# Attention and a mixing layer in one kernel: transposes moved from TensorE to VectorE blocks and DMAs

## Chip, cores and metric

The kernel runs on one core of a Trainium2 chip. The metric is the device time of one execution in microseconds (us). Its engines are TensorE (PE; its weight loads are shown as PEld), VectorE (DVE), ScalarE (ACT), GpSimd (POOL) and SyncE (SP), which issues nearly all DMAs. Each engine takes its instructions strictly in order.

## What is computed

Eight batches, eight heads, 1152 keys and 576 pooled queries of 64 numbers. The attention's output, put together to 576 x 512 for each batch, is x of a mixing layer:

```python
q_pool = q.reshape(B, H, S // 2, 2, D).mean(axis=3)
scores = scale * np.matmul(q_pool, k.transpose(0, 1, 3, 2))
scores = scores - np.max(scores, axis=-1, keepdims=True)
attn = np.exp(scores)
attn = attn / (np.sum(attn, axis=-1, keepdims=True) + 1e-09)
x = np.matmul(attn, v)            # then (B, 576, 512)

theta = x @ w_theta               # 512 x 512
zr, zi = x * np.cos(theta), x * np.sin(theta)
y = einsum('ts,bsd->btd', w_tok_r, zr) + einsum('ts,bsd->btd', w_tok_i, zi)
u = x + y
return u + np.maximum(u @ w_ch, 0.0)
```

q, k and v are 32-bit, the four weight matrices 64-bit floating point; products are formed from a high and a low part of each operand (three products each).

## The kernel before

**First part (attention).** The work is cut into 32 pairs (a batch and two heads). For a pair, `load_q`, `load_k` and `load_v` bring the inputs, `prep_t` transposes keys and pooled queries on TensorE, `prep_hi` (ScalarE) and `prep_lo` (VectorE) split them. `maxpass` and `max_tail` form rough scores with a product of the high parts, and VectorE reduces each to its maximum: queries lie in four blocks of 128 with both heads side by side, and the last 64 queries of both heads in one tile `tail`. `max_nm` takes the maxima's negative, `max_row` transposes them on TensorE and copies them to `mT`, and `load_max` puts them by four DMAs into one row `nmr` for each head. `escore` then forms the exact scores with that row added, ScalarE takes the exponential into `pc`, `ssum` adds those up on GpSimd, `av` multiplies with `vn`, and `norm_sum` to `norm_store` divide by the sum (through DRAM, to spread a row over the partitions) and store the transposed x of the pair to `xd`. Between these steps a generator, `weights`, reads the four weight matrices, which arrive as 64-bit floating point, and converts them piece by piece (`narrow`, then `square` or `token`), nine steps a pair at `W_AT`.

**Second part (mixing).** For each of eight batches `xload` brings the transposed x (512 x 576, in four chunks `c`), with the last 64 columns twice, so that the tokens fill five tiles `j` of 128. `xhi` and `xlo` split it. For each tile `xturn` transposes x back on TensorE (four transposes into the bank pxn), `theta` forms twelve products, and `chain` makes cosine and sine of it in eight steps on ScalarE and VectorE, multiplies them with x, and splits the result into Z (nine tiles; the last holds cosine and sine of the last 64 tokens). `token_mix` forms y in two groups of chunks, `uadd`, `uhi` and `ulo` make u, `channel` and `relu` the last product for the output's chunk `e`. The result stands transposed in `uT`; `oturn` transposes it on TensorE (four transposes into po for each of five tiles), `ocopy` copies it out and `ostore` writes it.

**Order.** Everything is put on a list with a position and sorted: in the first part in units of one score step (18 a pair, `PLAN`, `PREP_AT`, `MAX_AT`, `W_AT`), in the second in units of about a microsecond (56 a batch, `THETA_AT`, `CHAIN_AT`, `TOK_AT`, `CH_AT`, `OT_AT`). Each engine, SyncE too, takes its instructions in this order. In the first part all PSUM tiles share four slots of two banks that `bank2` gives out by a forecast (`HOLD`); in the second there is one bank each for theta (`h`) and for transposes (`t`), four `m` and two `r`. A tile with several buffers waits until the last user of the buffer is through.

Of the kernel before, what the change touches and what calls it, by code (L numbers as in the profile page):

```python
# [20 lines left out]
MAX_AT = (-25.08, -24.951, -24.126, -21.989, -17.714, -16.703, -16.481, -16.035, -13.864, -10.761, -9.027, -7.903)  # L21
SS_LAG = 5.493
AV_AT = (((10.593, 9),), ((19.957, 9),))
PREP_AT = {'t0': -34.901, 'hi0': -34.757, 'px': -9.4, 'lo0': -34.733, 't1': -26.381, 'hi1': -26.225, 'lo1': -25.86, 'tail': -25.662, 'row': -7.096}
NS_AT = 29.431
AV_WORK = 0.49
W_FIRST = (9.45, 9.5, 9.85, 10.5, 12.75, 18.0, 18.6, 19.25, 20.45)
W_AT = (4.835, 9.561, 10.424, 11.959, 14.518, 18.485, 19.386, 19.73, 26.978)
W_LAST = (9.4, 10.2, 11.0, 11.8, 12.6, 13.4, 14.2, 15.0, 15.8, 16.6, 17.4, 18.2, 19.0, 19.8, 20.6, 21.4, 22.2, 23.0, 23.8, 24.6)
W_END = 30  # L30
PRO = ((-34.75, -25.8, -18.2), (-6.0, -5.0, 3.15), (3.75,))
MAX_AT0 = (-25.75, -25.25, -24.75, -24.25, -24.15, -23.25, -22.0, -21.95, -21.75, -21.25, -20.75, -20.25)
MAX_AT1 = (-18.663, -17.319, -17.013, -16.938, -15.662, -12.596, -12.521, -11.476, -9.96, -9.477, -8.761, -8.295)
PLAN = {'load_q': -55.68, 'load_k': -42.082, 'pool_q': -40.682, 'load_max': -4.09, 'load_v': 0.076, 'max_nm': -7.805, 'norm_spread': 33.352, 'norm_load': 35.388, 'norm_recip': 37.458, 'norm_save': 39.746, 'norm_bcast': 45.007, 'norm_out': 46.788, 'norm_store': 60.302}
# [3 lines left out]
HOLD = {'e': (3.508, 'a', 0.849), 'pm': (0.312, 'd', 2.851), 'pt': (8.399, 'ad', 1.03), 'px': (2.27, 'd', 2.445), 'pa': (8.509, 'a', 2.216), 'mt': (3.434, 'a', 1.931), 'ns': (2.931, 'a', 0.172), 'pw': (1.991, 'ad', 0.781)}  # L38
# [8 lines left out]
XN0_BANK = "tmmrt"  # L47
# [21 lines left out]
OT_AT = (57.8, 60.7, 61.2, 63.0, 68.5)  # L69
OT_LAG = 1.0  # L70
# [12 lines left out]
def pooled_attention_moe_kernel(  # L83
# [49 lines left out]
    xd = [dram.tile([DM, SQ], F32, name=f"xd{b}") for b in range(B)]  # L133

# [44 lines left out]
    def xhi(b, c):  # L179
        if b == 0:  # L180
            nc.vector.tensor_copy(xhl[0][c], bst[b]["xT"][:, c])
        else:
            nc.scalar.copy(xhl[0][c], bst[b]["xT"][:, c])

    def xlo(b, c):
        getattr(nc, ENG2["xlo0" if b == 0 and c < ND - 1 else "xlo"]).tensor_tensor(
            xhl[1][c], bst[b]["xT"][:, c], xhl[0][c].bitcast(F32), ALU.subtract
        )

    with ExitStack() as p1:  # L190
# [107 lines left out]
        def maxpass(i):  # L298
# [4 lines left out]
            for j in range(4):  # L303
                for g in range(3):
                    pm = bank2("pm", f"pm{i}_{j}{g}")
                    for h, hs in enumerate(HEADS):
                        nc.tensor.matmul(  # L307
                            pm[:, h, 0:W],
                            hi[hs, Q0 + j * P : Q0 + (j + 1) * P],
# [12 lines left out]
                    if rest:  # L322
                        nc.vector.tensor_reduce(mx[:, 8, 2:3], pm[:, 0, W:], AX.X, ALU.max)
                    yield

        def max_tail(i):
# [3 lines left out]
            for n, c, k, w in ((0, 0, 0, 4), (1, 0, 4, 2), (1, 2 * P, 6, 2)):  # L330
                nc.tensor.matmul(  # L331
                    pm[:, n, c : c + w * P], tl, hi[:, K0[k] : K0[k] + w * P], start=True, stop=True
                )
            nc.vector.tensor_reduce(mx[:, 8, 0:2], pm, AX.X, ALU.max)

        def max_nm(i):
            st = state[i]
            nm = st["nm"] = sml.tile([P, KT], F32, tag="nm", name=f"nm{i}")
            nc.vector.tensor_reduce(nm, st["mx"], AX.X, ALU.max, negate=True)

        def max_row(i):
            st = state[i]
            px = bank2("mt", f"pmt{i}")
            nc.tensor.transpose(out=px[0:KT, 0, 0:P], in_=st["nm"], identity=ident)
            mT = st["mT"] = sml.tile([KT, P], F32R, tag="mT", name=f"mT{i}")
            nc.scalar.copy(mT, px[0:KT, 0, 0:P])
# [304 lines left out]
        def plan(i):  # L651
# [10 lines left out]
            if i == 0:  # L662
                at(-7.8, 3, max_row, i)
# [340 lines left out]
```

## Time and profile before

| | before |
|---|---|
| three runs | 1379.57 us median (1379.42 to 1379.85) |
| the profiled execution | 1378.9 us |
| its span, first to last instruction | 1377.1 us |
| TensorE busy | 1336.4 us (97%), 12178 products |
| VectorE, ScalarE, GpSimd busy | 840.2, 699.2, 910.8 us |
[...]
| DMA | 132057 packets, 111.66 MB |

The first part ends about 873 us into the span. A row of the profile names the line of the kernel, the engine, the operation, and the tiles as out<-in. In a timeline the first number is the start and the second the time from the first start to the last end of the merged instructions, in us; TensorE's products are pipelined and their ends are modelled, so lengths are best read from one start to the next.

### The profile page before, as it was taken

How to read it: one execution, taken by the hardware profiler on the slowest of the kernel's cores; microseconds unless marked ns; L12 is line 12 of the kernel's file. 1: busy time of each engine (PE TensorE's matmuls, PEld its weight loads, DVE VectorE, ACT ScalarE, POOL GpSimd, SP SyncE). 2: the span in 40 equal slices, each digit the busy share in tenths (PEclk: the TensorE clock that was granted, in tenths of full speed). 3: DMA queues.
4: the chain of work that ended last, by engine and by line, in shares of the span. 5: the costliest groups of instructions: out<-in, count | busy, mean ns of one | idle time of the engine just before them, and what ended most of it. 6: DMA issues, size and time to landing. Idle time of an engine off the chain costs nothing.

```text
span 1377.1 us, 29856 instructions
## 1 busy us (share of the span) xinstructions
PE 1336.4 (97%) x12178; PEld 1087.0 (79%) x12178; DVE 840.2 (61%) x1143; ACT 699.2 (51%) x1250; POOL 910.8 (66%) x672
## 2 busy tenths in 40 slices
PE   4999999999999999999999999899999999999998
PEld 3777777777777777677677777588999999999998
DVE  5767776677767676777667765366254353625442
ACT  1556555565555655556555565365454444445341
POOL 1699899899989899889988989553241323323220
PEclk9999999999999999999999999999999999999999
DMA  4333433434433344243443313211121111111011
GB/s 104 101 95 105 124 96 92 129 95 105 122 103 103 96 130 105 74 126 95 120 120 99 88 52 103 74 70 39 36 60 52 36 39 35 39 35 52 23 35 35
DMA packets 132057, 111.66 MB, mean 81 GB/s; under 512 B 96192, under 2 KB 96576, under 8 KB 131920
## 3 DMA queue, kind: packets, MB, share of 16 engines
q1 hardware_dynamic: 131744, 109.29, 29.2%
q8 instruction: 96, 1.57, 0.5%
q0 software_dynamic: 176, 0.46, 0.1%
q14 instruction: 41, 0.34, 0.1%
HBM read 88.30 MB, written 21.27 MB: 80 GB/s over the span
## 4 chain that ended last, share of the span: by engine, by line
PE 82%; DVE 6%; ACT 5%; POOL 4%; issue 1%; DMA 1%; SPq 0%; POOLq 0%; ACTq 0%; DVEq 0%
PE pe L372 21%; PE pa L398 19%; PE py L834 11%; PE pth L756 7%; PE pm L307 7%; PE pr L873 6%; PE pt L267 4%; POOL ss L384 3%; PE pns L419 2%; PE px L331 1%; DVE mx L319 1%; PE pxn L744 1%; DVE r L778 1%; DVE r L779 1%; PE po L896 1%
## 5 line engine op out<-in xcount | busy, mean ns | idle before, releaser
L384 POOL TENSOR_TENSOR ss<-ss,pc 128x576 f32<-128x576 f32 x384 | 557.4, 1452 | 47.3 <-ACT pc L375 21.3
L319 DVE TENSOR_REDUCE mx<-pm 128x2 f32<-128x768 f32 x384 | 360.9, 951 | 184.2 <-PE pm L307 167.1
L375 ACT ACTIVATE pc<-pe 128x576 f32<-128x576 f32 x576 | 343.7, 654 | 82.6 <-PE pe L372 77.4
L398 PE MATMUL pa<-pc,vn 128*64 128x288 f32 x2304 | 293.5, 409 | 4.3 <-ACT tail L290 2.2
L807 POOL TENSOR_TENSOR Z<-ab,Z 128x512 fp32r<-128x512 f32 x40 | 51.6, 1291 | 310.2 <-ACT Z L803 267.8
L398 PEld LDWEIGHTS pa<-pc,vn 128*64 128x64 f32 x2304 | 159.7, 137 | 115.8 <-issue 5.9
L834 PE MATMUL py<-wtk,Z 128*128 128x288 f32 x1728 | 242.0, 297 | 0.0
L834 PEld LDWEIGHTS py<-wtk,Z 128*128 128x128 f32 x1728 | 233.2, 189 | 1.5 <-ACT Z L803 0.2
L372 PE MATMUL pe<-hi 64*128 64x288 f32 x1152 | 177.9, 301 | 0.7 <-DVE wtk L166 0.3
L372 PE MATMUL pe<-nmr,oner 64*128 64x288 f32 x1152 | 172.7, 291 | 2.9 <-DMA nmr<-mT 2.9
L372 PE MATMUL pe<-hi,lo 64*128 64x288 f32 x1152 | 173.2, 292 | 0.0
L372 PE MATMUL pe<-lo,hi 64*128 64x288 f32 x1152 | 173.0, 293 | 0.0
L307 PE MATMUL pm<-hi 64*128 64x384 f32 x768 | 146.6, 389 | 5.7 <-DVE mx L319 2.3
L372 PEld LDWEIGHTS pe<-hi 64*128 64x128 f32 x1152 | 110.7, 185 | 10.8 <-issue 6.5
L410 ACT COPY xu<-pa 128x288 f32<-128x288 f32 x64 | 25.6, 399 | 178.8 <-PE pa L398 178.8
L372 PEld LDWEIGHTS pe<-nmr,oner 64*128 64x128 f32 x1152 | 111.5, 185 | 3.2 <-DMA nmr<-mT 3.1
L307 PEld LDWEIGHTS pm<-hi 64*128 64x128 f32 x768 | 72.6, 188 | 51.3 <-issue 28.3
L372 PEld LDWEIGHTS pe<-hi,lo 64*128 64x128 f32 x1152 | 111.2, 185 | 0.0
L372 PEld LDWEIGHTS pe<-lo,hi 64*128 64x128 f32 x1152 | 110.9, 185 | 0.0
L873 PEld LDWEIGHTS pr<-us,wch 128*128 128x128 f32 x768 | 104.4, 188 | 2.0
L873 PE MATMUL pr<-us,wch 128*128 128x288 f32 x768 | 105.6, 295 | 0.0
L384 POOL TENSOR_TENSOR ss<-pc,pc 128x576 f32<-128x576 f32 x64 | 94.3, 1473 | 6.6 <-ACT pc L375 6.6
(97 smaller groups left out, 1659.0 us busy)
## 6 DMA issues: line engine op xcount, KB each, us to landing
qn<-in_q_dram SPq DMA_DIRECT2D x32, 576.0 KB
kn<-in_k_dram SPq DMA_DIRECT2D x64, 288.0 KB
vn<-in_v_dram SPq DMA_DIRECT2D x32, 576.0 KB
dn<-ro SPq DMA_DIRECT2D x64, 144.0 KB
xd<-xu SPq DMA_DIRECT2D x32, 288.0 KB
xT<-xd SPq DMA_DIRECT2D x8, 1152.0 KB
out_dram<-on SPq DMA_DIRECT2D x23, 192.0 KB
out_dram<-on SPq DMA_DIRECT2D x23, 128.0 KB
```

What stands on the lines that cost most here:

```text
L267: nc.tensor.transpose(out=pt[:, n, c : c + R], in_=src.rearrange("p h d -> p (h d)"), identity=ident[0:R, 0:R],)
L307: nc.tensor.matmul(pm[:, h, 0:W], hi[hs, Q0 + j * P : Q0 + (j + 1) * P], hi[hs, K0[3 * g] : K0[3 * g] + W], start=True, stop=True,)
L319: nc.vector.tensor_reduce(mx[:, j : j + 5 : 4, g : g + 1], pm[:, :, 0:W], AX.X, ALU.max)
L372: nc.tensor.matmul(pe[:, h, 0:HALF], w[hs], x[hs], start=(n == 0), stop=(n == 3))
L375: nc.scalar.activation(pcs[u, kt], pe[:, :, 0:HALF], AF.Exp, scale=SC)
L384: nc.gpsimd.tensor_tensor(st["ss", u], first, st["pc"][u, kt], ALU.add)
L398: nc.tensor.matmul(pa[hs, 0, 0:HALF], st["vn"][:, h, kt, :], st["pc"][u, kt][:, h, :], start=(kt == 0), stop=(kt == KT - 1),)
L419: nc.tensor.matmul(px[a : a + 32, 1, 0:HALF], ones, sets[u][n][:, h, :], start=(n == 0), stop=(n == len(sets[0]) - 1), tile_position=(0, a),)
L756: nc.tensor.matmul(th, xs[c][:, j * P : (j + 1) * P], ws[:, c], start=(n == 0), stop=(n == 11))
L807: engine("zlo", b).tensor_tensor(Z[1], t, Z[0].bitcast(F32), ALU.subtract)
L834: nc.tensor.matmul(st["py", c, u][:, 0:HALF], Z[zi][:, c * P : (c + 1) * P], wtk[wi][:, kw, u * HALF : (u + 1) * HALF], start=(i == 0 and ...
L873: nc.tensor.matmul(pr[u][:, 0:HALF], wch[wi][:, c, e * P : (e + 1) * P], st["us", ui][:, c, u * HALF : (u + 1) * HALF], start=(n == 0), st ...
```

## The change

- The second part's transposes of x: each pair's finished x is also transposed on VectorE in blocks of 32 x 32 (`norm_turn`, tile `xb`) and stored to a second DRAM buffer `xbd`. `xnload` reads it from there with four DMAs for a tile, whose pieces are 32 words (128 bytes) long, straight into `xn`. `xturn` and the copies of its bank are gone.
- The output's transposes: for all batches but the last, `oblock` transposes each finished chunk `e` on VectorE in blocks (28 times) and stores it with four DMAs of 128-byte pieces. `oturn`, `ocopy` and `ostore` stay for the last batch.
- theta's last tile holds 64 tokens of an even batch and 64 of the odd one behind it. It is formed in the even batch; its angle is kept in `r4`, and two DMAs make a copy with the halves changed over (`r4s`). In odd batches `theta` returns at once for j = 4, and high and low parts are made for 512 columns.
- The maxima: the query blocks are taken with a step of four, so that `load_max` can read the row straight from `nm`, four words a partition. `max_row` (a transpose, a ScalarE copy) is gone. The product of the tail with the last keys moves from the last step of `maxpass` to `max_tail`, in a PSUM tile of its own.
- Weights: in `narrow` two VectorE passes are gone; ScalarE does one pass more. Ten steps a pair instead of nine, and the transposes of `token` have a place of their own (`TURN_AT`).
- All positions of the first part and the forecast of its PSUM slots are new. Positions of the second part stay, but for the removed and added steps.

```diff
@@ first part, places
-MAX_AT = (-25.08, -24.951, -24.126, -21.989, -17.714, -16.703, -16.481, -16.035, -13.864, -10.761, -9.027, -7.903)
-SS_LAG = 5.493
+MAX_AT = (-25.047, -24.524, -21.303, -19.913, -17.966, -17.199, -16.59, -13.533, -11.031, -9.109, -7.944, -7.783)
+SS_LAG = 5.544
...
-PLAN = {'load_q': -55.68, 'load_k': -42.082, 'pool_q': -40.682, 'load_max': -4.09, 'load_v': 0.076, 'max_nm': -7.805, 'norm_spread': 33.352, 'norm_load': 35.388, 'norm_recip': 37.458, 'norm_save': 39.746, 'norm_bcast': 45.007, 'norm_out': 46.788, 'norm_store': 60.302}
+PLAN = {'load_q': -54.727, 'load_k': -43.238, 'pool_q': -43.609, 'load_max': -3.244, 'load_v': -11.696, 'max_nm': -7.412, 'norm_spread': 32.09, 'norm_load': 34.755, 'norm_recip': 36.124, 'norm_save': 36.922, 'norm_bcast': 37.251, "norm_out": 46.61, "norm_turn": 46.640, 'norm_store': 56.838}
...
-XN0_BANK = "tmmrt"
+XN_AT = -4.0
...
-OT_AT = (57.8, 60.7, 61.2, 63.0, 68.5)
-OT_LAG = 1.0
+OB_LAG = 0.1
@@ xload
-        nc.sync.dma_start(xT[:, :, SQ : 5 * P], xv[:, :, 4 * P : SQ])
+        if b % 2 == 0:
+            xw = xd[b + 1].rearrange("(c p) s -> p c s", p=P)
+            nc.sync.dma_start(xT[:, :, SQ : 5 * P], xw[:, :, 4 * P : SQ])
+
+    def xwide(b):
+        return slice(0, 4 * P if b % 2 else 5 * P)
@@ maxpass
-                            hi[hs, Q0 + j * P : Q0 + (j + 1) * P],
+                            hi[hs, Q0 : Q0 + 4 * P].rearrange("d (p j) -> d j p", j=4)[:, j],
...
-                    rest = j == 3 and g == 2
-                    if rest:
-                        nc.tensor.matmul(
-                            pm[:, 0, W:], st["tail"], hi[:, K0[8] : K0[8] + P], start=True, stop=True
-                        )
...
-                    if rest:
-                        nc.vector.tensor_reduce(mx[:, 8, 2:3], pm[:, 0, W:], AX.X, ALU.max)
@@ max_tail
+            py = bank2("py", f"py{i}")
+            nc.tensor.matmul(py[:, 0, 0:P], tl, hi[:, K0[8] : K0[8] + P], start=True, stop=True)
             nc.vector.tensor_reduce(mx[:, 8, 0:2], pm, AX.X, ALU.max)
+            nc.vector.tensor_reduce(mx[:, 8, 2:3], py[:, 0, 0:P], AX.X, ALU.max)
@@ max_row goes; load_max
-                nc.sync.dma_start(row[:, 0 : 4 * P], mT[4 * h : 4 * h + 4])
-                nc.sync.dma_start(row[:, 4 * P : SQ], mT[8:9, h * HT : (h + 1) * HT])
+                nc.sync.dma_start(row[:, 0 : 4 * P], nm[:, 4 * h : 4 * h + 4])
+                nc.sync.dma_start(row[:, 4 * P : SQ], nm[h * HT : (h + 1) * HT, 8:9])
@@ new, and norm_store
+        def norm_turn(i):
+            st = state[i]
+            xb = st["xb"] = nrm.tile([P, SQ], F32, tag="xb", name=f"xb{i}", bufs=1)
+            nc.vector.transpose(xb, st["xu"].rearrange("p u c -> p (u c)"))
...
+            nc.sync.dma_start(xbd[b][hp * P : (hp + 1) * P, :], state[i]["xb"])
@@ narrow
-                nc.vector.tensor_scalar(f, lo, 8, None, ALU.logical_shift_right)
-                yield
-                nc.scalar.activation(tl, f, AF.Copy, scale=2.0**-44)
-                nc.vector.tensor_scalar(f, hi, 0x7FFFFFFF, None, ALU.bitwise_and)
+                nc.scalar.activation(tl, lo, AF.Copy, scale=2.0**-52)
+                nc.scalar.activation(f.bitcast(F32), hi.bitcast(F32), AF.Abs)
@@ xturn becomes
+        def xnload(b, j):
+            st = bst[b]
+            xn = st["xn", j] = ang.tile([P, DM], F32, tag="xn", name=f"xn{b}_{j}")
+            xv = xbd[b].rearrange("(c t) (n s) -> n t c s", t=32, s=32)
+            for n in range(4):
+                src = xv[4 * j + (n if j < 4 else n % 2)]
+                nc.sync.dma_start(xn[32 * n : 32 * n + 32].rearrange("p (c s) -> p c s", s=32), src)
@@ theta
+            if b % 2 and j == 4:
+                return
@@ chain (odd batches skip the first three steps for j = 4)
+                r2 = tmp("r2") if j < 4 else r4
...
+                if j == 4:
+                    nc.sync.dma_start(r4s[HT:P], r4[0:HT])
+                    nc.sync.dma_start(r4s[0:HT], r4[HT:P])
...
+                rc, rs = (r4s, r4) if b % 2 else (r4, r4s)
+                nc.scalar.activation(ab[0:HT], rc[0:HT], AF.Abs)
...
-                nc.scalar.activation(ab[HT:P], r2[HT:P], AF.Sin)
+                nc.scalar.activation(ab[HT:P], rs[HT:P], AF.Sin)
@@ new
+        def oblock(b, e):
+            st = bst[b]
+            ub = up.tile([P, SQ], F32, tag="ub", name=f"ub{b}_{e}")
+            nc.vector.transpose(ub, st["u"][:, e])
+            ov = out[b].rearrange("(n i t) (e a s) -> e a i t n s", n=3, t=QT, a=4, s=32)
+            for a in range(4):
+                nc.sync.dma_start(
+                    ov[e, a], ub[32 * a : 32 * a + 32].rearrange("i (t n s) -> i t n s", t=QT, n=3)
+                )
@@ the second part's list
-                at2(t, xturn, b, j)
+                at2(t + XN_AT, xnload, b, j)
...
+                if b < B - 1:
+                    at2(base + CH_AT[e] + RELU_LAG + OB_LAG, oblock, b, e)
-            for j in range(5):
-                t = base + OT_AT[j]
+            for j in range(5 if b == B - 1 else 0):
```

## Rows read from the trace of the kernel before

**Rows 1.** Stretches: length, then busy PE, PEld, DVE, ACT, POOL; clock, DMA share, GB/s.

```profile
120.00:300.00 180.00, 179.29 (x1894) 132.55 (x1892) 128.41 (x160) 102.81 (x189) 162.54 (x119) 1.00 0.40 106
...
860.00:880.00 20.00, 14.74 (x150) 9.11 (x149) 8.66 (x7) 5.32 (x11) 19.22 (x13) 0.97 0.28 90
1000.00:1100.00 100.00, 99.39 (x684) 94.05 (x683) 47.32 (x82) 46.70 (x79) 33.14 (x24) 1.00 0.17 50
```

**Rows 2.** Timeline of TensorE over a batch of the second part.

```profile
1038.85 0.60 PE L744 MATMUL pxn<-ident,xT 128*128 128x128 f32 x4
...
1082.09 1.76 PE L834 MATMUL py<-wtk,Z 128*128 128x288 f32 x12
...
1099.45 0.60 PE L744 MATMUL pxn<-ident,xT 128*128 128x128 f32 x4
1099.80 2.10 PE L756 MATMUL pth<-wth,xh 128*128 128x512 f32 x8
1101.74 1.09 PE L756 MATMUL pth<-wth,xl 128*128 128x512 f32 x4
1102.67 8.15 PE L834 MATMUL py<-wtk,Z 128*128 128x288 f32 x60
1110.66 0.60 PE L744 MATMUL pxn<-ident,xT 128*128 128x128 f32 x4
```

**Rows 3.** Timeline of TensorE in the first part.

```profile
403.24 4.59 PE L398 MATMUL pa<-pc,vn 128*64 128x288 f32 x36
407.75 0.45 PE L307 MATMUL pm<-hi 64*128 64x384 f32 x2
...
409.62 0.34 PE L307 MATMUL pm<-hi 64*128 64x384 f32 x2
409.79 0.30 PE L372 MATMUL pe<-hi 64*128 64x288 f32 x2
...
415.61 0.33 PE L316 MATMUL pm<-hi,tail 128*128 128x128 f32 x1
415.87 4.58 PE L398 MATMUL pa<-pc,vn 128*64 128x288 f32 x36
420.38 0.28 PE L344 MATMUL pmt<-ident,nm 128*9 128x128 f32 x1
420.59 0.44 PE L307 MATMUL pm<-hi 64*128 64x384 f32 x2
420.87 0.29 PE L372 MATMUL pe<-hi 64*128 64x288 f32 x2
```

**Rows 4.** Groups by line and shape: VectorE in the weights' conversion (busy, mean ns).

```profile
L527 DVE TENSOR_SCALAR wf<-raw 128x576 uint32<-128x576 uint32 x8 | 6.0, 747 | 3.0 <-POOL ss L384 3.0
L534 DVE TENSOR_SCALAR wf<-ws 128x576 uint32<-128x576 uint32 x8 | 6.0, 746 | 0.1
```

**Rows 5.** DMA queue (packets, MB, share): 414.8-418.5, 405.5-406.9, 1121.9-1127.5 us.

```profile
q1 hardware_dynamic: 2078, 0.53, 64.6%
...
q1 hardware_dynamic: 144, 0.00, 6.6%
...
q1 hardware_dynamic: 1056, 1.31, 73.6%
```

**Rows 6.** Timelines of the other engines, and the group of one ScalarE copy.

```profile
1121.91 0.38 SPq L176 DMA_DIRECT2D xT<-xd  x1
...
442.44 0.94 SPq L506 DMA_DIRECT2D raw<-in_moe_w_ch_dram  x1
...
1136.34 0.82 DVE L886 SCALAR_TENSOR_TENSOR uT<-pr,uT 128x288 f32<-128x288 f32 x2 [1.32 <-PE pr L873]
...
1087.61 1.98 ACT L183 CAST xh<-xT 128x640 fp32r<-128x640 f32 x3
...
1088.54 6.14 POOL L186 TENSOR_TENSOR xl<-xT,xh 128x640 fp32r<-128x640 f32 x4
...
L783 ACT COPY xn<-pxn 128x512 f32<-128x512 f32 x35 | 20.4, 582 | 0.0
```

More of the change, by code (lines that the diff above doesn't have):

```diff
@@ L133, in pooled_attention_moe_kernel @@
     xd = [dram.tile([DM, SQ], F32, name=f"xd{b}") for b in range(B)]
+    xbd = [dram.tile([DM, SQ], F32, name=f"xbd{b}") for b in range(B)]
     def bank(kind, name):
@@ L585, in token, with turn @@
                 yield
-                yield
-                yield
+                turns.append(lambda: turn(ws, kb, jt, R))
+                while turns:
+                    yield
+            def turn(ws, kb, jt, R):
                 pw2 = bank2("pw", "pwt")
@@ L625, in weights, with turn_next @@
                         yield from group[n]
+        def turn_next():
+            while turns:
+                turns.pop()()
         def early():
-            run(wgen)
+            while not run(wgen, 20):
+                turn_next()
             pw.close()
@@ L693, in plan @@
                 ("norm_out", norm_out),
+                ("norm_turn", norm_turn),
                 ("norm_store", norm_store),
@@ L700, in pooled_attention_moe_kernel @@
         pw = ExitStack()
+        turns = []
         wgen = weights()
@@ L723, in pooled_attention_moe_kernel @@
         xhl[1].append(xp.tile([P, 5 * P], F32R, name=f"xl{ND - 1}"))
+        r4 = xp.tile([P, DM], F32, name="r4")
+        r4s = xp.tile([P, DM], F32, name="r4s")
         wcp = p2.enter_context(tc.tile_pool(name="wcp", bufs=1))
@@ L738, in wload @@
                 nc.sync.dma_start(wch[n].bitcast(F32), wcd[n].rearrange("c p e -> p c e"))
-        def xturn(b, j):
+        def xnload(b, j):
             st = bst[b]
-            pt = st["xn", j] = bank(XN0_BANK[j] if b == 0 else "t", f"pxn{b}_{j}")
-            for c in range(ND):
-                nc.tensor.transpose(
-                    out=pt[:, c * P : (c + 1) * P],
-                    in_=st["xT"][:, c, j * P : (j + 1) * P],
-                    identity=ident,
-                )
+            xn = st["xn", j] = ang.tile([P, DM], F32, tag="xn", name=f"xn{b}_{j}")
[3 more added lines that the diff above has]
+                nc.sync.dma_start(xn[32 * n : 32 * n + 32].rearrange("p (c s) -> p c s", s=32), src)
         def theta(b, j):
+            if b % 2 and j == 4:
+                return
             st = bst[b]
@@ L904, in ocopy @@
             R = P if j < 4 else HT
-            if b < B - 1 or j < 2:
-                on = up.tile([P, DM], F32, tag="on", name=f"on{b}_{j}")
-            else:
-                on = ang.tile([P, DM], F32, tag=("kk", "r2", "xn")[j - 2], name=f"on{b}_{j}")
-            st["on", j] = on
+            tag = ("kk", "r2", "xn", "ab", "ti")[j]
+            on = st["on", j] = ang.tile([P, DM], F32, tag=tag, name=f"on{b}_{j}")
             if b == B - 1 and j % 2:
```

84 lines of the change are left out of this document (39 added, 45 removed).

## Prediction

> **What bounds the kernel now.** I read the busy times by stage first [rows 1]. In the first part (attention, 32 head pairs) TensorE is busy 179.29 of 180 us, and GpSimd with 162.54 is the next; in the second part (eight batches of mixing) TensorE is busy 99.39 of 100 us, no other engine reaches half, and the DMA engines are used to 0.17. Only the change between the parts has a hole (860 to 880 us: 14.74 busy). So a TensorE instruction taken out is worth its whole length, as long as nothing that was hidden below TensorE comes to light. The view to read next is therefore TensorE's own order of time, at the places where the instructions in question stand [rows 2, 3]; then the other queues, for the cover that is left [rows 4 to 6]. The profiled execution took 1378.9 us, its span is 1377.1 (1.8 lie around it); the median of the three runs is 1379.57, 0.7 above. The sum is made against 1378.9.
>
> **Second part: what leaves TensorE.** The output's transposes (po): a batch lasts 60.6 us (1038.85 to 1099.45), and from its first token product at 1082.09 to the transposes at 1099.45 are 17.36 [rows 2], in which 108 token products and the five po groups stand. Sixty such products without anything between them take 1110.66 - 1102.67 = 7.99, so 0.133 each and 14.38 for 108. The five groups, with their waits for the copy out of PSUM, cost 2.98 a batch; in seven batches (the last one keeps them) 20.9 us.
> The input's transposes (pxn): a group takes 1099.80 - 1099.45 = 0.35, and the theta products right behind it are slower: eight in 1.94 (0.2425 each), the next four in 0.93 (0.2325), which is 0.08 more. 40 groups by 0.43: 17.2 us.
> Theta's half tile: twelve products are 1102.67 - 1099.80 = 2.87, without the 0.08 already counted 2.79; four odd batches lose them: 11.2 us. Together 49.3 us.
>
> **First part: what leaves TensorE.** The transpose of the maxima (pmt) lies between 420.38 and 420.59; the products ahead of it take 4.51 (415.87 to 420.38), as they do where a maxima product follows them directly (403.24 to 407.75) [rows 3]. So all its 0.21 goes, 32 times: 6.7 us. The single product with the tail (L316) takes 0.26 (415.61 to 415.87) and moves behind the three other tail products (L331), where 128 more columns cost at least 0.06 (128/288 of 0.133) and at most the 0.26; I take 0.12, twice the least, since its weights are loaded anew. 32 times 0.14: 4.5 us. Together 11.2, and with the second part 60.5: 1318.4 us if all else stays hidden.
>
> **What is added.** (a) The maxima's weights are now read with a step of four words (16 bytes). Within a run of score products a maxima step costs 0.17 (409.62 to 409.79); behind a change of the array's tiling it costs 0.28 (420.59 to 420.87) [rows 3]. The 0.11 between them is one load of 128 columns of weights that nothing hides. If the step makes a load last twice as long, it shows with 0.11 behind a change, and within a run with 0.22 less the 0.13 of the product that hides it, 0.09: for 384 steps about 38 us. If it costs nothing, 0. No gain is possible, since the same bytes are loaded. The nearest rows are VectorE reading words with a step of 8 bytes and without one: 747 and 746 ns [rows 4], no cost. They are near the lower end, but not at 16 bytes, so I take a tenth of the upper end, 4 us.
> (b) VectorE's transposes, 32 in the first and 28 in the second part, are not in this trace. A VectorE pass over as many columns, two by 288, takes 0.82 [rows 6]; I take 0.8 each, and 1.6 as the upper end. In the second part that is 3.2 (6.4) a batch on an engine that is idle half of the time. In the first part it is 0.8 in a pair of 26 us on an engine that is busy 128.41 of 180, and the weight conversion gives up two passes of 0.75 in 18 of these pairs [rows 1, 4]. Nothing is added to the sum: TensorE waits on VectorE mostly through PSUM banks, and the average room is over 7 us a pair.
> (c) The DMAs. One batch reads 20 by 512 and writes 16 by 576 pieces of 128 bytes, 19,456 in all. Pieces of 256 bytes keep an engine busy 0.646 x 3.7 us x 16 / 2078 = 18.4 ns each, pieces of 36 bytes that go to HBM 0.066 x 1.4 x 16 / 144 = 10.3 ns [rows 5]. So 128 bytes cost 10 to 18 ns, and a batch 12.5 to 22 us of 16 engines, in the 54 us that a batch now lasts (60.6 less 6.5). That is hidden.
> (d) SyncE's queue. 36 or 38 issues a batch, at 0.38 to 0.94 each [rows 6], are 14 to 36 us of 54. What counts is the order. The load of x for the batch after next, issued at 1121.91 as soon as its buffer is free, now stands behind the stores of the first three output blocks, and each of these waits for its relu and its transpose. From the end of the third relu (1136.34 + 0.82 = 1137.16) to theta's first product with the low part of that x, one batch on at 1101.74 + 60.6 = 1162.3, are 25.1 us [rows 2, 6]; of these 2.98 + 2 x 0.43 = 3.8 go with the transposes, and 2.8 more where the half tile is skipped: 21.3 or 18.5 are left. In them must lie 0.8 for the transpose, six issues at 0.38 to 0.94 (2.3 to 5.6), the transfer (its 1056 packets fit into the 5.6 us from 1121.9 to 1127.5 [rows 5]), and casts and low parts on ScalarE and GpSimd, 7.1 us from 1087.61 to 1088.54 + 6.14: 15.8 to 19.1. Hidden, with 2 to 5 us of room after even batches, but only -0.6 to 2.7 after odd ones: the thinnest cover here.
> (e) Behind the half tile's angle two DMAs move its halves, and ScalarE waits for one of them in even batches: some 2 us, with the casts of the next x behind it on ScalarE. Its product is the last of nine that TensorE takes, 12.8 us into the batch. Hidden; the ScalarE copies that go, ten a batch at 0.58 [rows 6], more than pay.
> (f) The row of maxima: the four DMAs move small pieces (16 and 4 bytes), but are issued when VectorE has the maxima, ahead of the transposed copy that they waited for. Between nothing and 0.5 us a pair; nothing, since the lead grows by what the transpose and its copy took.
> For (c) to (e) I allow 0.5 us a batch that does come to light, 4 us. **Sum:** 1378.9 - 60.5 + 4 + 4 = 1326.4, so 1326.
>
> **Rivals.** *The stepped weights show in full.* Then 1326 - 4 + 38 = 1360. For it: a load has only 0.02 to spare below a score product (0.13 against 0.11). Against it: nothing stepped costs anything in [rows 4], and two reads are not as near as one would like.
> [...]
> *A new wait in the second part.* The load of x or the natural copies of x come late: 3 us in each of six batches at the place in (d), and up to 3 at the start, where the third tile of batch 0 has to wait for a buffer: about 20, so 1346. For it: five queues keep their old order while TensorE runs 10% faster past them. Against it: the room worked out in (d), of which only the upper end of the issue time leaves nothing.
> *The pieces become the bound, and the kernel gets slower.* The place is the 16 DMA engines in the second part. From 54 x 16 / 19,456 = 44 ns a piece they set the pace of a batch; from about 50 ns (60.6 + 1.4 us a batch) the gain of both parts is gone; at 60 ns a batch takes 73 us and the kernel 1326 + 8 x 19 = 1478. For it: rows 2 KB apart in HBM are written in pieces. Against it: 10.3 and 18.4 ns in [rows 5], three times below.
> [...]
> *The change does not do what it says:* the new places in the first part cost what the part saves, or the groups leave idle time in TensorE instead. All 52 us would have to be lost.
>
> **How the numbers follow.** Forecast, with partly hidden weights and small waits, 0.55 (1315 to 1337 by itself); stepped weights in full or in good part 0.22; new waits 0.16; pieces 0.05; no effect 0.02. The lower end, 1315, is 1318.4 less the 3 us that TensorE idles in the first part (0.71 in 180, over some 820 us [rows 1]); the upper end reaches the stepped weights, 1358. A measurement of this kernel tells 0.2%, 2.8 us, from no change. Faster takes the first three cases and little else: 0.94; same 0.01; slower 0.05.
>
> **What would show it.** po gone from seven batches, pxn from all and the theta group from odd ones: a batch of about 54.0 us between two first token products, 52.6 and 55.4 in turn. TensorE busy over 99% in the second part; if it is less, the name behind the wait says which cover broke: xl or xh (d), Z of the half tile (e), an xn DMA on VectorE (c). Maxima steps of 0.17 and 0.28 stay if the stepped load is free and become about 0.26 and 0.39 if it is doubled. DMA share in the second part 0.35 to 0.5; near 1 would be the slow pieces. What would make the prediction wrong is first (a), then (d).

## The result, and the profile after

The changed kernel takes 1324.72 us (median of four runs, 1322.45 to 1325.5), the kernel before, on the same chip, 1379.49 (1378.67 to 1379.85): 0.9601 of it, with an interval of 0.9584 to 0.9618. The forecast was 1326. The profiled execution has a span of 1322.9 us, against 1377.1 before.

The stretches of [rows 1], in the profile of after:

```profile
120.00:300.00 180.00, 178.39 (x1879) 139.73 (x1877) 130.97 (x162) 102.93 (x185) 168.26 (x123) 1.00 0.45 120
860.00:880.00 20.00, 16.61 (x124) 11.67 (x121) 4.14 (x5) 5.50 (x10) 11.93 (x9) 0.91 0.26 66
1000.00:1100.00 100.00, 100.00 (x680) 95.63 (x679) 53.12 (x91) 41.71 (x68) 32.21 (x24) 1.00 0.38 71
```

TensorE is still what bounds both parts (178.39 of 180, 100.00 of 100). In the first part GpSimd has come nearer, 168.26 of 180. In the second part the DMA share has gone from 0.17 to 0.38. The hole between the parts is still there (16.61 of 20 us busy, 14.74 before).

The two traces are now cut at the same four places. Before, the first token products of batch 0, of batch 1 and of the last batch on TensorE's timeline:

```profile
899.94 21.99 PE L834 MATMUL py<-wtk,Z 128*128 128x288 f32 x162
...
960.94 1.77 PE L834 MATMUL py<-wtk,Z 128*128 128x288 f32 x12
...
1324.45 1.76 PE L834 MATMUL py<-wtk,Z 128*128 128x288 f32 x12
```

After, with two batches in the middle:

```profile
888.39 9.74 PE L852 MATMUL py<-wtk,Z 128*128 128x288 f32 x72
...
947.85 14.56 PE L852 MATMUL py<-wtk,Z 128*128 128x288 f32 x108
...
1003.35 14.56 PE L852 MATMUL py<-wtk,Z 128*128 128x288 f32 x108
...
1056.07 14.56 PE L852 MATMUL py<-wtk,Z 128*128 128x288 f32 x108
...
1272.51 28.96 PE L852 MATMUL py<-wtk,Z 128*128 128x288 f32 x216
```

| stretch | before | after | measured | my sum |
|---|---|---|---|---|
| start to the first token product | 899.94 | 888.39 | -11.55 | -11.2 - 5 x 0.43 (pxn of batch 0) + 4 (a) = -9.35 |
| batch 0 | 61.00 | 59.46 | -1.54 | -5 x 0.43 - 2.79 = -4.94 |
| the next six batches | 363.51 | 324.66 | -38.85 | -6 x 5.13 - 3 x 2.79 = -39.15 |
| last batch to the end of the span | 52.65 | 50.39 | -2.26 | -2.98 |
| allowance for (c) to (e) | | | | +4 |
| span | 1377.1 | 1322.9 | -54.2 | -52.4 |

(The output of one batch is transposed in the next one, so batch 0 has no po, and the last has that of its predecessor.) From batch 1 on the second part went as worked out; batch 0 gained less. The stretch with the first part comes out near the sum too, but not by its terms, as the rows of the maxima show (after, the whole run):

```profile
L315 PE MATMUL pm<-hi 64*128 64x384 f32 x768 | 173.8, 464 | 4.4 <-ACT hi L291 2.1
...
L315 PEld LDWEIGHTS pm<-hi 64*128 64x128 f32 x768 | 118.0, 306 | 35.3 <-issue 26.0
```

In the window 120 to 820 us the load's row has 306 ns after, and 183 before:

```profile
L307 PEld LDWEIGHTS pm<-hi 64*128 64x128 f32 x634 | 58.1, 183 | 37.7 <-issue 24.5 <-DVE mx L319 2.7 <-DVE ws L532 0.9
```

On the timeline of [rows 3], now of after:

```profile
404.62 0.43 PE L315 MATMUL pm<-hi 64*128 64x384 f32 x2
404.89 0.29 PE L369 MATMUL pe<-hi 64*128 64x288 f32 x2
...
411.36 4.59 PE L395 MATMUL pa<-pc,vn 128*64 128x288 f32 x36
415.88 0.56 PE L315 MATMUL pm<-hi 64*128 64x384 f32 x2
416.28 0.29 PE L369 MATMUL pe<-hi 64*128 64x288 f32 x2
```

A maxima step between score products takes 0.27 us (404.62 to 404.89; 0.17 in [rows 3]), one behind another tiling 0.40 (415.88 to 416.28; 0.28 before). The forecast said "about 0.26 and 0.39 if it is doubled". So the stepped load does show as a doubled one (0.12 more behind another tiling, on the 0.11 of the forecast), and still the sum held. What that hides is the question of the experiments.

One more working was made from the starts of all TensorE products of 25 pairs (130.99 to 792.65 us before, 121.66 to 776.48 after): the time from each product's start to the next one's start, put to the first of the two, in us a pair.

| | pm | pe | pa | pt | px and the tail product | pmt | pwt | pns | sum |
|---|---|---|---|---|---|---|---|---|---|
| before | 3.01 | 10.04 | 9.03 | 1.78 | 0.92 | 0.21 | 0.34 | 1.14 | 26.47 |
| after | 3.81 | 9.68 | 9.06 | 1.64 | 0.71 | 0 | 0.19 | 1.11 | 26.19 |
| difference | +0.79 | -0.36 | +0.03 | -0.14 | -0.21 | -0.21 | -0.15 | -0.03 | -0.27 |

### The profile page after: what moved, and what is told of

Read it like the earlier page. It is cut to its first block, busy times and chain, and to the rows that moved or that the text cites. A ratio compares the mean times of both kernels' runs of the same rounds, so it can differ in the third digit from the quotient of the medians.

```text
span 1322.9 us, 29392 instructions
## 1 busy us (share of the span) xinstructions
PE 1288.2 (97%) x11798; PEld 1082.7 (82%) x11798; DVE 848.9 (64%) x1151; ACT 663.5 (50%) x1157; POOL 907.7 (69%) x672
## 4 chain that ended last, share of the span: by engine, by line
PE 88%; DVE 4%; ACT 3%; POOL 2%; DMA 2%; issue 1%; SPq 0%; POOLq 0%; ACTq 0%; DVEq 0%
PE pe L369 21%; PE pa L395 20%; PE py L852 15%; PE pm L315 8%; PE pr L891 7%; PE pth L767 7%; PE pt L275 4%; PE pns L416 3%; DVE mx L322 2%; POOL ss L381 2%; PE px L332 1%; DMA xn<-xbd 1%; ACT pc L372 1%; ACT Z L821 0%; DMA kn<-in_k_dram 0%
## 5 line engine op out<-in xcount | busy, mean ns | idle before, releaser
L852 PE MATMUL py<-wtk,Z 128*128 128x288 f32 x1728 | 236.0, 297 | 0.7 <-ACT Z L821 0.5
L315 PE MATMUL pm<-hi 64*128 64x384 f32 x768 | 173.8, 464 | 4.4 <-ACT hi L291 2.1
L369 PE MATMUL pe<-hi 64*128 64x288 f32 x1152 | 173.8, 296 | 3.2 <-ACT pc L372 1.7
L315 PEld LDWEIGHTS pm<-hi 64*128 64x128 f32 x768 | 118.0, 306 | 35.3 <-issue 26.0
L407 ACT COPY xu<-pa 128x288 f32<-128x288 f32 x64 | 25.6, 400 | 213.4 <-PE pa L395 213.4
```

The lines of the kernel that those rows point to most:

```text
L315: nc.tensor.matmul(pm[:, h, 0:W], hi[hs, Q0 : Q0 + 4 * P].rearrange("d (p j) -> d j p", j=4)[:, j], hi[hs, K0[3 * g] : K0[3 * g] + W], sta ...
L369: nc.tensor.matmul(pe[:, h, 0:HALF], w[hs], x[hs], start=(n == 0), stop=(n == 3))
L852: nc.tensor.matmul(st["py", c, u][:, 0:HALF], Z[zi][:, c * P : (c + 1) * P], wtk[wi][:, kw, u * HALF : (u + 1) * HALF], start=(i == 0 and ...
```

## Experiments

**Theory and rivals.** Theory A: the maxima's stepped weights cost tens of microseconds, and something else in the first part gave as much back. Theory B: the step is almost free, as my sum had it. For the second part: the sum's terms are the real ones, and the cover of the load of x is as thin as I said.

### The step alone, in the kernel before

```diff
-  hi[hs, Q0 + j * P : Q0 + (j + 1) * P],
+  hi[hs, Q0 : Q0 + 4 * P].rearrange("d (p j) -> d j p", j=4)[:, j],
```

> The kernel before with one edit: the maxima's weights are read with a step of four words. The row of maxima is left as it was, so each maximum goes to another query (the softmax divides it out again). Theory A, a stepped load takes twice as long: 6 steps a pair behind score products by 0.10 to 0.115, four behind another tiling by 0.12, two that stand together by 0.10: about 1.2 a pair, 39 us, so 1418 (1405 to 1422, as some of it may fall into waits that the pairs of before have: 25.86 us the shortest, 26.5 the mean). My forecast's term (a): 1384. Step free: 1379.5.

Measured: 1415.1 us against 1378.07, a ratio of 1.0265 (1.025 to 1.0281): 37.0 us more. The sums' copy stands once in a pair on ScalarE, so its first and last start give the mean pair, here in the window 140 to 820 us. Before, and with the step:

```profile
L428 ACT ACTIVATE sm<-pns,eps x25: 500/501/503, 158.6 to 793.9; 128x288 f32<-128x288 f32 x25
```

```profile
L428 ACT ACTIVATE sm<-pns,eps x24: 500/502/503, 163.8 to 800.9; 128x288 f32<-128x288 f32 x24
```

(793.9 - 158.6) / 24 = 26.47 us a pair, and (800.9 - 163.8) / 23 = 27.70: 1.23 more, 39 us in 32 pairs. Theory A's number, and nearly my upper end for term (a), 38.

### Which steps cost

```diff
+  ws = [hi[hs, Q0 : Q0 + n * P].rearrange("d (p j) -> d j p", j=n)[:, 0] for n in (2, 3, 4, 6)]
   (one matmul line for each j, with ws[j])
```

> The changed kernel, but the four groups of maxima products read their weights with steps of 2, 3, 4 and 6 words (8, 12, 16, 24 bytes), each on a line of its own. Left out: the right place of each maximum, and with the step of 6 also some keys are taken for queries. Without a step the load's row has 188 ns on average (before), with a step of four words 306 (after). [...] If any step doubles the load: 306 for all. If the time goes with the bytes that are spanned: 250, 280, 306, 350 or more. [...]

The loads' rows by line (steps of 2, 3, 4 and 6 words are lines 321, 323, 325 and 327), window 120 to 820 us:

```profile
L325 PEld LDWEIGHTS pm<-hi 64*128 64x128 f32 x162 | 25.6, 306 | 0.0
...
L327 PEld LDWEIGHTS pm<-hi 64*128 64x128 f32 x162 | 24.1, 300 | 0.0
...
L323 PEld LDWEIGHTS pm<-hi 64*128 64x128 f32 x162 | 20.6, 249 | 12.3 <-issue 10.5 <-PE pa L401 1.8
...
L321 PEld LDWEIGHTS pm<-hi 64*128 64x128 f32 x162 | 15.8, 191 | 11.8 <-issue 11.8
```

Two words: 191 ns, little more than without a step (183 in the same window). Three: 249, about halfway between 183 and 306. Four and six: 306 and 300. So neither of the two expectations holds: not every step costs the same, and the time doesn't go with the bytes spanned. It rises between two words and four and is no higher with six; why, no run shows. The kernel took 1314.19 us, 10.5 less than after.

### Taking the step away from the changed kernel

```diff
-  hi[hs, Q0 : Q0 + 4 * P].rearrange("d (p j) -> d j p", j=4)[:, j],
+  hi[hs, Q0 + j * P : Q0 + (j + 1) * P],
-  nc.sync.dma_start(row[:, 0 : 4 * P], nm[:, 4 * h : 4 * h + 4])
+  for j in range(4):
+      nc.sync.dma_start(row[:, j * P : (j + 1) * P], nm[:, 4 * h + j : 4 * h + j + 1])
```

> The changed kernel with the maxima's weights read without a step again; the row is put in order by its DMAs instead, which move single words (4 bytes, 1,152 a pair in ten DMAs instead of 384 pieces in four). Theory A, a stepped load takes twice as long: in the trace of after a maxima step costs 0.277 us behind score products and 0.403 behind another tiling, before it was 0.177 and 0.28. Without the step the old costs come back, 8 x 0.10 + 2 x 0.12 + 0.10 for the two that stand together = 1.14 a pair, 32 pairs: 36 us, so about 1288; the load's row falls from 306 to about 190 ns. Theory B, the step is free and only the record of the load is longer (my forecast had 4 us): 1320 to 1325. Theory C, TensorE gives it back to GpSimd, which is busy 168 of 180 us in the first part, or to the maxima's row, which comes later by the 4-byte pieces: 1300 to 1312, with waits for ss, pc or nmr in TensorE's rows.

And the same weights, with the row put in order by VectorE:

```diff
+  nt = st["nt"] = sml.tile([P, 32], F32, tag="nt", name=f"nt{i}")
+  nc.vector.transpose(nt, nm.bitcast(F32))      # nm is 128x32 now, 9 columns used
   load_max: five DMAs for each head, pieces of 32 words out of nt
```

> As the kernel with single words, but the row is put in order by one more transpose of 32x32 blocks on VectorE (128x32) and ten DMAs of 128-byte pieces. Theory A (a stepped load takes twice as long): within 3 us of the kernel with single words, about 1288, since only the way of the row differs. If the single words are what delays the row (theory C, its second half), this one is faster than the other by more than 5 us. Theory B (the step is free): 1320 to 1327.

Measured: 1313.26 and 1310.51 us. The ratios are 0.9531 (0.9515 to 0.9548) and 0.9504 (0.9489 to 0.952). So 11.5 and 14.2 us come back, not 36; the 2.7 between the two ways of the row are no more than their intervals. The load's rows are 183 and 184 ns in the same window, as before. TensorE's waits in the second of them, 120 to 820 us (total, times, longest), then the groups of the first score products and of VectorE's maxima in the same window, and the stretch of [rows 1]:

```profile
PE pe L378 <- DVE mx L324: 3.7, 5, 1.1
PE pe L378 <- ACT pc L381: 2.2, 4, 0.7
```

```profile
L378 PE MATMUL pe<-hi 64*128 64x288 f32 x978 | 155.9, 315 | 6.5 <-DVE mx L324 3.7 <-ACT pc L381 2.2 <-DVE lo L304 0.6
L324 DVE TENSOR_REDUCE mx<-pm 128x2 f32<-128x768 f32 x327 | 305.7, 956 | 158.4 <-PE pm L317 157.6
```

```profile
120.00:300.00 180.00, 176.59 (x1925) 134.36 (x1923) 137.83 (x171) 106.97 (x190) 172.39 (x126) 1.00 0.45 121
```

In the working by starts pm falls from 3.81 to 2.75 us a pair (34 us in 32 pairs), but pe grows from 9.68 to 10.20. GpSimd is at 172.39 of 180, and the scores wait for VectorE's maxima, which hold PSUM slots. Either could take the gain; two runs look at one each.

```diff
-  nc.gpsimd.tensor_tensor(st["ss", u], first, st["pc"][u, kt], ALU.add)
+  eng = nc.vector if u == 1 and kt == 1 else nc.gpsimd
+  eng.tensor_tensor(st["ss", u], first, st["pc"][u, kt], ALU.add)
```

> The kernel with contiguous weights and the row by VectorE's transpose (1310.51 us), with one of the 14 additions of a pair (1.43 us on GpSimd) on VectorE. Why did taking the step away bring 14 us and not 36? In that kernel the maxima's rows on TensorE fell by 1.05 us a pair, but the score rows grew from 9.68 to 10.20; GpSimd is busy 172.4 of 180 us, and ScalarE waits for its additions to give exponentials' buffers back. Theory: GpSimd is the bound, mean pair 25.64, shortest 25.02. With the addition moved the mean pair comes to 25.1 to 25.3, and the kernel to 1295 to 1303. Rival: the order of the PSUM slots, planned for the stepped loads, holds the rest (waits of the scores for VectorE's maxima): 1308 to 1312, or slower, as VectorE (76%) gets 1.4 us a pair more.

Measured: 1312.89 us (1309.01 to 1315.32), no gain over 1310.51. GpSimd did get its relief:

```profile
120.00:300.00 180.00, 175.97 (x1915) 133.83 (x1915) 138.57 (x178) 106.41 (x189) 159.82 (x117) 1.00 0.46 124
```

159.82 of 180, and the pairs stay at (816.5 - 149.7) / 26 = 25.65 us, by the sums' copies from 140 to 820 us. VectorE's busy time from 120 to 820 us went from 522.49 to 536.31 us for it, 0.5 a pair. So room on GpSimd alone brings nothing; whether VectorE took back what GpSimd gave, the next run tells.

```diff
-  mx[:, j : j + 5 : 4, g : g + 1], pm[:, :, 0:W], AX.X, ALU.max
+  mx[:, j : j + 5 : 4, g : g + 1], pm[:, :, 0 : W // 2], AX.X, ALU.max
```

> The kernel with contiguous weights and VectorE's transpose of the maxima (1310.51 us), in which VectorE takes each maximum over half of the columns only. Left out: the other half, so that the value taken off before the exponential is not the true maximum (the division takes it out again). Taking the step away brought 14 of some 36 us; moving 1.43 us a pair from GpSimd to VectorE brought nothing. What is left as the cause: PSUM slots that VectorE's maxima (0.956 us each, 12 a pair) hold against the next scores; TensorE's named waits are for DVE mx (3.7 us) and ACT pc (2.2), and pe's first products last 315 ns on average instead of 294. Theory: with maxima of about half the time the mean pair comes from 25.64 to 24.7 to 25.1, where GpSimd (24.0 us busy a pair) is next, and the kernel to 1290 to 1298. Rival: the slots go round in the planned order whatever VectorE does, and the exponentials' buffers hold the pair: 1306 to 1311.

Measured: 1288.95 us (1287.37 to 1290.03), 21.6 less than with whole maxima. The mean pair, with the step taken away, with whole and with half maxima:

```profile
L434 ACT ACTIVATE sm<-pns,eps x27: 500/500/501, 149.3 to 814.1; 128x288 f32<-128x288 f32 x27
```

```profile
L434 ACT ACTIVATE sm<-pns,eps x28: 501/502/502, 143.9 to 816.1; 128x288 f32<-128x288 f32 x28
```

```profile
L324 DVE TENSOR_REDUCE mx<-pm 128x2 f32<-128x384 f32 x324 | 178.6, 558 | 240.8 <-PE pm L317 233.4
L378 PE MATMUL pe<-hi 64*128 64x288 f32 x1008 | 151.7, 295 | 2.7 <-ACT pc L381 2.4 <-DVE mx L324 0.3
```

(814.1 - 149.3) / 26 = 25.57 us and (816.1 - 143.9) / 27 = 24.90; VectorE's maximum takes 558 ns instead of 956, and the first score product 295 instead of 315. GpSimd still does all 14 additions of a pair here, so it was not what held the pairs at 25.6. VectorE's maxima took the rest of the gain: 14 + 22 = 36 us, the price that theory A had named for the plain weights. Whether it is the slots that they hold or their share of VectorE's queue (137.83 of 180 us busy with whole maxima) this run doesn't separate.

Half maxima on the changed kernel, with its step, weren't run, so part of the 22 could have been there to gain without any change of the weights. The traces speak against it. In a pair in which TensorE has no idle time and no weights are transposed, the working by starts gives 25.77 us for the changed kernel, of which the score products pe take 9.57; without the step 25.01 and 10.0; with half maxima as well 24.51 and 9.54. So the undisturbed pairs of after hold no such wait, and the two falls (0.76 and 0.50) add up to 1.26, near the 1.23 that the step cost in the kernel before.

### The places of before

```diff
 MAX_AT, MAX_AT1, AV_AT, PREP_AT, NS_AT, SS_LAG, PLAN, HOLD: the values of before
+  HOLD["py"] = HOLD["px"];  PLAN["norm_turn"] = 46.818
```

> The changed kernel with the first part's places of before (maxima steps, tails, attention products, norm sums, loads, and the planner's costs of PSUM slots), but with the step of four words and without the transpose of the maxima's row. Theory A: the stepped loads cost over 1 us a pair and the new places give most of it back (in after 2 of 12 maxima steps stand behind another tiling, before 4, and pe's rows fall from 10.04 to 9.68 us a pair); with the old places the shortest pair takes 27.19 (the kernel before with the step) - 0.21 (pmt) - 0.2 (tail product) = 26.8 instead of 25.77, and the kernel 1350 to 1360. If the new places are worth nothing: 1325, with the shortest pair at 25.8.

Measured: 1455.99 us, far beyond the 1360. TensorE's longest waits between 120 and 820 us:

```profile
PE pa L395 <- ACT tail L298: 19.5, 7, 2.9
PE pm L315 <- DVE mx L322: 13.2, 10, 1.7
```

By the working of starts a pair takes 30.25 us here, with pm at 5.27, pe at 10.48, pa at 9.80 and the weights' transposes pwt at 1.13 (0.19 in after). The places of the weights' steps (`W_AT`, `TURN_AT`) stayed those of after, so this is no clean return to the old order. The planner gives out PSUM slots in the order of these places, and the new slot for the tail product (py) may put the others out of step; that isn't shown. The run prices no single thing. It shows only that the change doesn't stand with these places.

### The second part: the output's transposes given back to TensorE

```diff
-  at2(base + CH_AT[e] + RELU_LAG + OB_LAG, oblock, b, e)
+  oturn, ocopy, ostore for j in range(5), at OT_AT and OT_LAG of before
```

> The changed kernel with the output's transposes given back to TensorE in the first seven batches (po, its copy by ScalarE and its store, at the places of before), instead of VectorE's blocks of 32x32 and the DMAs of 128-byte pieces. If the first term of my sum is sized right, 2.98 us a batch come back: batches of 58.48 and 55.70 in turn (55.50 and 52.72 now), the kernel 1324.7 + 20.9 = 1345.6. If po's cost in before was its products alone (20 of about 0.09) and not its waits for the copies: 1.8 a batch, 1337. If the 128-byte pieces hold something up in after, less comes back than 12.

Measured: 1342.94 us, 18.2 more. Three starts of batches (the first token product of each):

```profile
949.29 1.76 PE L853 MATMUL py<-wtk,Z 128*128 128x288 f32 x12
...
1006.89 1.76 PE L853 MATMUL py<-wtk,Z 128*128 128x288 f32 x12
...
1062.97 1.76 PE L853 MATMUL py<-wtk,Z 128*128 128x288 f32 x12
```

57.60 and 56.08 us in turn, 2.1 and 3.4 more than in after; the mean, 2.73, is what po costs. I had 2.98. Its products alone (1.8) are too little.

### The thinnest cover

SyncE issues the load of x, GpSimd makes the low parts, TensorE takes them (after, an odd batch):

```profile
1057.86 0.57 SPq L177 DMA_DIRECT2D xT<-xd  x1
```

```profile
1065.84 6.15 POOL L194 TENSOR_TENSOR xl<-xT,xh 128x640 fp32r<-128x640 f32 x4 [4.65 <-ACT xh L190]
```

```profile
1072.34 1.09 PE L767 MATMUL pth<-wth,xl 128*128 128x512 f32 x4
```

```diff
-  "xload": -64.6
+  "xload": -59.5        # behind the fourth block's stores, not the third's
```

> The changed kernel, with the load of x for the batch after next one block of output stores later on SyncE: behind the fourth block instead of the third. It asks how much room is left in the cover that my forecast called the thinnest (term (d): 2 to 5 us after even batches, -0.6 to 2.7 after odd ones). In the trace of after the load is issued at 1057.86, GpSimd has the last low part at 1071.99, and TensorE takes the first product with it at 1072.34; after the other kind it is 1127.08 and 1127.84: 0.4 to 0.8 us of room, some 0.7 more for the fourth of the low parts. The four stores of the fourth block, with their wait for VectorE, take SyncE until about 1064.4, 5.3 to 6.6 us longer. Theory, the room is what the trace shows: TensorE waits 4 to 6 us for xl in each of six batches, 24 to 36 us in all: 1349 to 1361. If the queue has slack that the trace doesn't show (the transfer or the casts get faster when they start later): under 1335.

Measured: 1341.59 us, 16.9 more; less than expected, but the cover breaks at once:

```profile
PE pth L767 <- POOL xl L194: 11.6, 14, 1.5
```

The load is issued 4.70 us after the batch's first token product (1065.40, 1060.70) instead of 1.79 (1057.86, 1056.07). So the delay was 2.9 us and not the 5.3 to 6.6 that I took, and 2.9 is more than the room. All six later batches got longer, by 1.6 to 5.1 us.

### Start of the second part

```diff
-X1_AT = -4                      PLAN2["wload"] = 12.0
+X1_AT = -60                     PLAN2["wload"] = -59.0
```

> The changed kernel; on SyncE the load of x for batch 1 and that of the channel weights go ahead of the natural copies of batch 0 from its third tile on. In after the third of these waits for a buffer, and the load of x is issued only at 903.67 us; then TensorE waits 0.92 and 0.73 us for xl and 1.07 for r, and the granted clock is 0.73 from 915 to 920: batch 0 takes 59.46 us where others of its kind take 52.72. Theory: the queue's order is the cause; the waits for xl and the clock's 1.7 us go, batch 0 takes 55 to 56.5, the kernel about 1321.5. Rival: the chain of batch 0 is the bound of this stretch, or the 2 MB of weights now delay the third natural copy; batch 0 stays at 59 to 61, the kernel 1324 to 1327.

Measured: 1334.66 us, 9.9 more. The waits for xl are gone, and in their place stands one of 10.55 us:

```profile
895.94 0.92 SPq L749 DMA_DIRECT2D wch<-wcd  x2
896.91 12.91 SPq L757 DMA_DIRECT2D xn<-xbd  x12
```

```profile
908.00 14.44 PE L852 MATMUL py<-wtk,Z 128*128 128x288 f32 x90 [10.55 <-ACT Z L821]
```

The 2 MB of channel weights (line 749) go out 0.97 us ahead of the rest of batch 0's natural copies (line 757), and TensorE waits for the Z that are made from those.

```diff
-  nc.gpsimd.tensor_tensor(st["ss", u], first, st["pc"][u, kt], ALU.add)
+  eng = nc.vector if i == NPAIR - 1 and u == 1 else nc.gpsimd
```

> The changed kernel, with the sums of the last pair's second half (7 of its 14 additions) on VectorE instead of GpSimd. In after TensorE waits for ss 2.80 us at 849 and 2.73 at 868, then 0.66 for the sums' copy, with a granted clock of 0.91 from 840 to 880. Theory: GpSimd, busy 168 of 180 us, is behind when the first part ends; 7 x 1.46 = 10 us taken from it at the end bring the first theta product forward by 2.7 to 4 us: 1321 to 1322. Rival: the last exponentials are late and not the additions: 1324 to 1325.

Measured: 1322.27 us (1320.9 to 1324.0), a ratio of 0.9592 (0.9578 to 0.9606); the interval reaches into that of after, so the time alone doesn't settle it. In the trace the first theta product comes at 869.25 instead of 872.79, as expected, and the first token product at 883.28 instead of 888.39; batch 0 gives 1.6 us of that back (61.06 for 59.46), with a wait of 3.3 for Z. The waits for xl fall from 1.7 to 0.7, with the load of x in its old place.

Together, with contiguous weights, and with the channel weights left in their place:

```diff
 contiguous weights, VectorE's transpose of the maxima; last pair's second half of sums on VectorE
-X1_AT = -4
+X1_AT = -60
```

> Contiguous weights with VectorE's transpose of the maxima, the last pair's second half of additions on VectorE, and SyncE's load of x for batch 1 ahead of the third natural copy of batch 0, but the channel weights where they are in after (their 2 MB were what the earlier reordering pushed ahead of the natural copies: TensorE waited 10.5 us for Z there). From 1310.5: the last pair's sums 2.5 to 4, the load of x 1.5 to 3.5: 1303 to 1307. If batch 0's chain holds instead (9 us of waits for Z and r): 1308 to 1311.

Measured: 1307.12 us (1306.93 to 1307.5), 0.9482 of before (0.9467 to 0.9498): 17.6 us less than the changed kernel, with all of the work done. Against 1310.51 it is 3.4, with intervals that overlap a little. The first theta product moves from 858.75 to 854.43 and the first token product from 874.76 to 868.46; batch 0 gives 2.4 back (61.93 for 59.52). Its rows of waits from 840 us on:

```profile
PE py L862 <- ACT Z L831: 2.7, 2, 2.4
PE pth L777 <- DVE r L800: 2.1, 1, 2.1
PE pth L777 <- POOL xl L194: 0.7, 1, 0.7
```

The waits for xl are 0.7 instead of 1.6, but they were 0.7 too with the last pair's sums alone, so it isn't shown that the load's new place took anything off them. The chain of batch 0 (Z, r) is what is late there now.

## Why the prediction was right, and where it was not

**po, pxn, theta's half tile: right.** Batches of 55.50 and 52.72 in turn, where 55.4 and 52.6 were forecast; 54.11 on average, for 54.0. The half tile is their difference, 2.78 (forecast 2.79). po is 2.73 (2.98), so by subtraction pxn is 60.58 - 54.11 - 1.39 - 2.73 = 2.35 (2.15): the split between the two was off by 0.2, their sum by 0.05.

**pmt and the tail product: right.** -0.21 and -0.21 us a pair in the working by starts, for -0.21 and -0.14.

**(a), the stepped weights: wrong, and the step that failed is the choice between its ends.** The bounds held: 0 to 38, and 37.0 measured in the kernel before. I took a tenth of the upper end, since VectorE's rows with a step of 8 bytes "are near the lower end". The run with four steps shows that 8 bytes cost TensorE next to nothing too (191 ns for 183), and that 16 cost the full price (306), no more than 24 do (300): TensorE's price rises between two and four words, and a row with a step of two could not tell of it. What VectorE pays for a longer step no run shows. The rival of the stepped weights was right for this term, and the 0.22 given to it too little.

**Why the time came out all the same.** In the rows of after, pm costs 0.79 a pair more, 25 us where I had 4. Against that, pe, pt, pwt and pns give 0.68 a pair, 22 us that stand in no term of mine. Most of it is the order of the products. In pairs in which TensorE has no idle time and no weights are transposed (25.85 us before, 25.77 after), pe falls from 9.90 to 9.57 and pt from 1.78 to 1.60: 0.51 of the 0.68. Before, TensorE leaves the score products (pe and pm, one tiling) for products of other tilings six or seven times a pair, in after twice, as the new places put the others side by side. Three of these times the last score products ahead of it are pe, which take 0.22 us there instead of 0.13 ahead of a maxima step (before, in one pair):

```profile
597.05 0.29 PE L372 MATMUL pe<-nmr,oner 64*128 64x288 f32 x2
597.18 0.34 PE L307 MATMUL pm<-hi 64*128 64x384 f32 x2
...
597.75 0.29 PE L372 MATMUL pe<-nmr,oner 64*128 64x288 f32 x2
597.97 0.74 PE L331 MATMUL px<-hi,tail 128*128 128x512 f32 x3
```

In after there is no such place. That is 3 x 0.09 = 0.27 of pe's 0.33. In the same way two of the twelve maxima steps stand behind another tiling where it had been four, which is 0.12 each in pm. The forecast priced such a change itself (0.11, in its term (a)), but didn't count how many of them the new places save: it weighed these only as a risk ("cost what the part saves"), never as a gain. Two errors of some 21 us cancelled, so the 1326 is luck as far as these two go, and no proof of the first part's sum. What is left of the 0.68, some 0.17 (5 us), is mostly the weights' transposes, which wait less; whether the places or VectorE's two lighter passes of the weight conversion did that stays open. No run takes the new order alone away, as the one with the old places was too coarse; the 16 us of order are read from the two traces.

**What the step costs depends on what is late next.** 37 us where it is added to the kernel before, 14 where it is taken from the kernel after, 36 where VectorE's maxima are shortened as well (if that alone would bring the changed kernel nothing). VectorE's maxima were hidden behind TensorE's longer loads, and came to light as these went.

**(b) and (f): right.** VectorE's transposes take 778 and 779 ns (0.8 forecast):

```profile
L470 DVE STREAM_TRANSPOSE xb<-xu 128x576 f32<-128x576 f32 x32 | 24.9, 778 | 1.1
...
L912 DVE STREAM_TRANSPOSE ub<-uT 128x576 f32<-128x576 f32 x28 | 21.8, 779 | 1.8 <-DMA out_dram<-ub 0.9
...
L369 PE MATMUL pe<-nmr,oner 64*128 64x288 f32 x1152 | 172.1, 293 | 2.1 <-DMA nmr<-nm 2.1
```

TensorE waits 2.1 us in all for the row of maxima (the last of these rows).

**(c): right.** The share is 0.38 at 1000 to 1100 us, within the 0.35 to 0.5. In one batch of after (1003.35 to 1056.07 us) the trace has 17,483 packets of 128 bytes at 13.1 ns of engine time on average, within the 10 to 18 of the forecast. A byte costs 1.7 times as much in them as in the 2,048-byte packets of a batch before (121.5 ns each), and nearly five times as much in the 36-byte pieces of [rows 5] (10.3 ns each). The forecast's sum goes by the time of a piece and doesn't rest on that of a byte. The price stays hidden: TensorE has no idle time between 1000 and 1300 us (300.00 of 300 busy) and the batches have the forecast length, so the rival of slow pieces falls there.

**(d) and (e): hidden, as forecast.** SyncE has 37 and 41 issues in two batches in turn (those from 1003.35 and 1056.07 us), where I counted 36 or 38. In (d), GpSimd ends the low parts at 1065.84 + 6.15 = 1071.99, 0.35 us ahead of TensorE's first product with them, and the last of the four products that start at 1072.34 takes the last part some 0.7 later: about 1 us of room, within the -0.6 to 2.7 of the forecast for this kind. For the other kind the low parts end at 1127.08 and the product starts at 1127.84: with the same 0.7 about 1.5 us, less than the 2 to 5 forecast, so the cover was thinner there than worked out. ScalarE does wait for transfers in the second part, 3.4 us each for the exchanged halves where I had some 2:

```profile
ACT xh L190 <- DMA xT<-xd: 10.8, 2, 5.6
ACT ab L812 <- DMA r4s<-r: 10.2, 3, 4.0
```

None of it reaches TensorE. The 4 us of allowance were used elsewhere: batch 0 gained 1.54 where the sum has 4.94, at the start of the second part, where the rival of new waits had put up to 3 us. TensorE waits there 0.55 us for Z, 1.65 for xl and 1.07 for r, and the granted clock is 0.73 of full speed on average from 915 to 920 us (0.50 from 918 to 920), after TensorE had waited 0.92 and 0.73 us for xl just ahead of it. The third natural copy of batch 0 is one link of this (VectorE waits 2.3 us for it until 897.28), SyncE's queue behind it another, and the moves of that queue that were run took little or nothing off it. A rival that no run tests is the DMA engines themselves: with the load of x, 2 MB of channel weights and the natural copies together, their share is 1.05 and 1.09 in the two stretches of 5 us from 905 to 915, so here, unlike later, the transfers may have been late by their amount and not by their order.

## What to carry to other kernels

Bound an unknown cost from a row of the same engine with a step as long: one of four words took the row of a load of TensorE's weights from 183 to 306 ns here, while one of two words was all but free (191). A busy share near 100% does not say that the order of the work is tight: count how often a period changes the tiling (here six times out of the score products' tiling before, twice after) before calling new places neutral. A total that fits is not a test of its terms: cut both traces at the same places, and undo the doubtful term alone.

## What the runs showed of the hardware that was not expected

A load of 64x128 words of weights has a row of 183 to 191 ns with steps of one and two words, 249 with three, 306 with four and 300 with six; a maxima step with weights read four words apart takes 0.27 us between score products and 0.40 behind another tiling, 0.10 and 0.12 more than without. A transpose of a 128x32 tile by VectorE, which puts the row of maxima in order without any step, takes 212 ns.
